# A gated convolution and an ELU feed-forward layer on one core: the last rows of w_in are loaded once and doubled by TensorE

## The chip, the cores and the metric

The kernel runs on one NeuronCore of a Trainium2 chip. The metric is the device time of one execution in microseconds (us); lower is better. The engines are named as in the profile: PE (TensorE: matrix products; PEld is its loading of weights), DVE (VectorE), ACT (ScalarE), POOL (GpSimd) and SP (SyncE, which here only issues DMAs; SPq is its queue). SBUF is the memory that the engines work on, PSUM the one that TensorE writes into.

## The reference

```python
# 4 x 4096 tokens of 192 features, 8 heads of 24 features, 7 taps
w = softmax(weight_gen, axis=-1)          # [B, S, 8, 7], sum + 1e-9
out[b, s, h] = sum_k w[b, s, h, k] * x_pad[b, s + k, h]      # causal, 24 features a head
h = out.reshape(16384, 192) @ w_in        # [192, 2048], float64 in memory
g = where(h > 0, h, exp(min(h, 0)) - 1)   # ELU
return (g @ w_out).astype(float32)        # [2048, 192], float64 in memory
```

So each token's features are averaged over seven places with its own softmaxed weights, and the result goes through two matrix products with an ELU between them.

## The kernel before

**Blocks and tiles.** The 16384 tokens are cut into 32 blocks of 512. A block's convolution gives a 192 x 512 matrix (features by tokens, after transposes). The 192 features lie in four quarters of 48; of each quarter the first 32 rows ("A") fill 128 partitions, and the last 16 rows ("D") of the four quarters make 64 rows, which are held twice, so that they fill 128 partitions as well. The hidden dimension of 2048 is cut into 16 f-tiles of 128.

**Split numbers.** Each factor is split into a high and a low part (hi, lo) that TensorE multiplies in one pass each. For one f-tile, `f_tile` issues five matmuls of 512 columns into the PSUM tile h (L467: D lo by xd, A lo by x hi, A hi by x lo, D hi by xd, A hi by x hi), then ScalarE and VectorE form the ELU and split it (L474 relu, L476 exp, L478 VectorE's add and max into h, L481 hi, L483 lo, which is the last reader of h), and five more matmuls add the tile's share of the result into the PSUM tiles acc and accd (L496). The doubled D rows carry the token's hi part against one copy and its lo part against the other (`second`, L450 and L453: xr and xd).

**Weights.** w_in and w_out come as 64-bit floats, two 32-bit words each. `weights(f0, nf)` handles a piece: first two pieces of one f-tile, then seven of two ("pairs"). SP loads it into the tile raw: one DMA for the A rows (L297), four for the D rows of the four quarters, each written to two places (L299), one for w_out (L302). ScalarE takes the absolute value of the upper words (L308) and scales the lower ones (L311), VectorE clamps, shifts and ors (L314, L317, L320), GpSimd adds the lower words (L323): the tile m is then float32. ScalarE casts it into W as the hi part (L325, L327), GpSimd subtracts for the lo part (L334). All weights stay in W.

**Convolution.** `chunk` loads inputs and softmaxes the tap weights. Blocks 0 and 1 are summed by TensorE: VectorE makes seven products v (L390) and TensorE adds them with an identity matrix in plain float32 (L419). Later blocks are made by GpSimd alone (seven products, six sums; the last writes xc), and VectorE transposes the result (L444) and forms xlo and xd (L453).

**What sets the order.** The code first records every task with an engine, a cost and a due time (`Plan.add`), and then a list scheduler (`Plan.issue`) simulates the engines and writes the instructions out in that order; each engine runs its own in the order written. A ring is a fixed number of buffers (h has 4, raw 4, m 3), and a task that takes a buffer waits until the previous holder's readers are through. The runs are block 0 with tiles 0 to 7, block 1 with 0 to 7, both with 8 to 15, then block 2 to 31 with all sixteen.

```python
runs = [(0, 0, NF2), (1, 0, NF2), (0, NF2, NF), (1, NF2, NF)]
runs += [(blk, 0, NF) for blk in range(2, NB)]
```

The names that the change touches: `weights`, the layout of W (A_HI ... D_LO), the rings raw, m and h, `f_tile` (which weights it waits for) and the constants at the start.

Of the kernel before, what the change touches and what calls it, by code (L numbers as in the profile page):

```python
# [141 lines left out]
def conv_elu_kernel(  # L142
# [38 lines left out]
    def rows(ap, t0, n):  # L181
# [26 lines left out]
    r_wm = ring("wm", [P, CM, H, 1], 1)  # L210
# [46 lines left out]
    def due1(s):  # L257
        return T0 + s * STEP
# [4 lines left out]

    def weights(f0, nf):
        raw, m, hi_h, lo_h = r_raw.new(), r_m.new(), Handle(), Handle()
        for f in range(f0, f0 + nf):
            w_h[f] = (hi_h, lo_h)
        n = nf * WC

        ni = 2 * nf * P  # L270

        def inputs(ap):
            return ap.rearrange("p (c f m) -> p c f m", c=2, f=nf)

        def outputs(ap):
            return ap.rearrange("p (f m) -> p f m", f=nf)

        def m_(c=slice(0, n)):
            return m.t[:, c]

        def mf(c=slice(0, n)):
            return m_(c).bitcast(F32)

        def word(i):
            return raw.t[:, 0:n, i]

        w_in, w_out = slice(0, ni), slice(ni, n)
        fs = W[:, f0:f0 + nf]
        in_hi = fs[:, :, 0:2 * P].rearrange("p f (c m) -> p c f m", c=2)
        in_lo = fs[:, :, A_LO.start:D_LO.stop].rearrange("p f (c m) -> p c f m", c=2)  # L290
        out_hi = fs[:, :, 2 * P:WC]

        def load():
            w = moe_w_in.bitcast(I32).rearrange("(q e) m -> q e m", q=Q)[
                :, :, 2 * f0 * P:2 * (f0 + nf) * P]
            r = raw.t[:, 0:n].rearrange("p c w -> p (c w)")
# [28 lines left out]
        add("act", act(ni), lambda: nc.scalar.copy(out=in_hi, in_=inputs(mf(w_in))),  # L325
            reads=[m], writes=[hi_h])
        add("act", act(n - ni), lambda: nc.scalar.copy(out=out_hi, in_=outputs(mf(w_out))),  # L327
            reads=[m], writes=[hi_h])
        for c, src, hi, lo in ((ni, lambda: inputs(mf(w_in)), in_hi, in_lo),
                               (nf * P, lambda: outputs(mf(w_out))[:, :, 0:P], fs[:, :, O_HI],  # L330
                                fs[:, :, O_LO]),
                               (nf * D1, lambda: outputs(mf(w_out))[:, :, P:D],
                                fs[:, :, O_BOTH.start:WC], fs[:, :, WC:O_BOTH.stop])):
            add("pool", pool(c), lambda src=src, hi=hi, lo=lo: nc.gpsimd.tensor_tensor(  # L334
                out=lo, in0=src(), in1=hi.bitcast(F32), op=ALU.subtract),
                reads=[m, hi_h], writes=[lo_h])

    xw_h, wg_h = {}, {}
# [118 lines left out]
    acc_h = {}  # L457

    def f_tile(blk, f, s, first, last):
        whi, wlo = w_h[f]  # L460
        xhi, xlo, xd, _ = xt_h[blk]
        h, e, hi, lo = r_h.new(), r_e.new(), r_hi.new(), r_lo.new()

# [29 lines left out]
        def mm2():  # L493
# [4 lines left out]
                    stop=(last and r is lo), skip_group_check=True,  # L498
                )

        add("pe", 5 * pe(N), mm2, reads=[whi, wlo, hi, lo], writes=[acc, accd],
            due=due1(s + LA) + 5 * pe(N))

    def drain(blk, s1):
# [30 lines left out]
    with tc.manual_schedule():  # L535

        nc.vector.memset(scratch, 0.0)
        nc.scalar.activation(out=scratch, in_=scratch, func=ACTF.Exp)
        make_identity(nc, ident)
        nc.gpsimd.iota(count, pattern=[[0, 1]], base=0, channel_multiplier=1)  # L540
        nc.vector.tensor_scalar(out=count, in0=count, scalar1=4, scalar2=1,
                                op0=ALU.logical_shift_right, op1=ALU.bitwise_and)
        nc.vector.tensor_copy(out=second, in_=count)
        s = 0
        for blk, f0, f1 in runs:
            c, j0 = chunk_of[blk]
# [46 lines left out]
```

## Time and profile before

| | |
|---|---|
| median of 3 runs | 1252.93 us (1252.63 to 1255.36) |
| the profiled execution | 1255.2 us, of which its span 1253.4 us |
| PE busy | 1200.1 us (96%) |
| DVE, ACT, POOL busy | 897.8, 914.8, 711.5 us (72%, 73%, 57%) |
| mean granted TensorE clock | 0.979 of full speed |

The span runs from the first instruction to the last; the execution's time holds some 2 us around it. Durations in the profile come from one execution. In a row of a timeline, the first number is the start in us from the span's start, the second the duration, and a bracket at the end gives the idle time of the engine before it and what ended it.

### The profile page before, as it was taken

The numbers are of one execution on the slowest core, as the hardware profiler recorded it, in microseconds if no ns is written. First come the engines' busy times: TensorE is split into PE (matmuls) and PEld (weight loads), VectorE is DVE, ScalarE is ACT, GpSimd is POOL, SyncE is SP. The second block draws the span as 40 slices with busy tenths as digits, with TensorE's granted clock in tenths as the row PEclk, the third lists the DMA queues.
The fourth block names the chain that finished last, engine by engine and source line by source line (L and its number), as shares of the span: only waits on it lengthen the run. The fifth ranks groups of instructions, "written<-read, shape, count | busy, mean of one in ns | idle before, by whom it ended". The sixth has DMA issues, their size and how long they took to land.

```text
span 1253.4 us, 15492 instructions
## 1 busy us (share of the span) xinstructions
PE 1200.1 (96%) x5176; PEld 980.1 (78%) x5176; DVE 897.8 (72%) x1398; ACT 914.8 (73%) x1687; POOL 711.5 (57%) x433
## 2 busy tenths in 40 slices
PE   3479999999999999999999999999999999999997
PEld 2248788788888888888888888888888888888886
DVE  5368878888778777676676777667776666666664
ACT  2258677778877777777777777777777777777775
POOL 2235999979999965646676464667656555000000
PEclk9679999999999999999999999999999999999999
DMA  4453040413331404030400403040140000000000
GB/s 102 106 101 44 15 49 13 50 14 45 42 40 24 51 13 51 13 38 13 50 13 13 50 14 44 7 51 13 15 49 13 7 7 13 13 13 13 13 14 13
DMA packets 252364, 39.69 MB, mean 32 GB/s; under 512 B 247932, under 2 KB 250492, under 8 KB 252284
## 3 DMA queue, kind: packets, MB, share of 16 engines
q1 hardware_dynamic: 252284, 38.70, 22.3%
q8 instruction: 40, 0.66, 0.2%
q14 instruction: 40, 0.33, 0.1%
HBM read 26.10 MB, written 12.58 MB: 31 GB/s over the span
## 4 chain that ended last, share of the span: by engine, by line
PE 88%; DMA 4%; SPq 3%; DVE 2%; ACT 2%; issue 1%; POOL 0%; ACTq 0%; POOLq 0%; DVEq 0%
PE h L467 44%; PE acc L496 26%; PE accd L496 18%; DMA raw<-in_moe_w_in 2%; SPq L359 2%; DMA raw<-in_moe_w_out 1%; ACT e L474 0%; SPq L299 0%; ACT e L476 0%; DVE h L478 0%; ACT hi L481 0%; DVE lo L483 0%; SPq L297 0%; POOL m L323 0%; SPq L302 0%
## 5 line engine op out<-in xcount | busy, mean ns | idle before, releaser
L483 DVE TENSOR_TENSOR lo<-h,hi 128x512 fp32r<-128x512 f32 x512 | 350.4, 684 | 291.3 <-ACT hi L481 284.9
L474 ACT ACTIVATE e<-h 128x512 f32<-128x512 f32 x512 | 305.9, 598 | 220.1 <-PE h L467 217.9
L467 PE MATMUL h<-xd,W 128*128 128x512 f32 x1024 | 403.9, 394 | 13.0 <-DVE xd L453 12.0
L496 PE MATMUL acc<-hi,W 128*128 128x512 f32 x1024 | 400.7, 391 | 15.7 <-ACT hi L481 15.7
L467 PE MATMUL h<-xhi,W 128*128 128x512 f32 x1024 | 401.4, 392 | 0.0
L478 DVE SCALAR_TENSOR_TENSOR h<-e,h 128x512 f32<-128x512 f32 x512 | 350.3, 685 | 21.9 <-ACT e L476 21.7
L481 ACT CAST hi<-h 128x512 fp32r<-128x512 f32 x512 | 298.3, 583 | 45.1 <-DVE h L478 43.3
L476 ACT ACTIVATE e<-e 128x512 f32<-128x512 f32 x512 | 329.1, 643 | 1.8
L390 POOL TENSOR_TENSOR pb<-xw,wg 128x768 f32<-128x768 f32 x180 | 284.6, 1581 | 13.9
L405 POOL TENSOR_TENSOR pa<-pa,pb 128x768 f32<-128x768 f32 x150 | 281.1, 1874 | 9.4
L467 PEld LDWEIGHTS h<-xd,W 128*128 128x128 f32 x1024 | 194.3, 190 | 57.1 <-issue 10.8
L496 PEld LDWEIGHTS acc<-hi,W 128*128 128x128 f32 x1024 | 192.9, 188 | 58.4 <-ACT hi L481 18.3
L467 PEld LDWEIGHTS h<-xhi,W 128*128 128x128 f32 x1024 | 194.4, 190 | 40.9 <-issue 0.6
L467 PE MATMUL h<-xlo,W 128*128 128x512 f32 x512 | 200.7, 392 | 0.0
L496 PE MATMUL accd<-lo,W 128*128 128x512 f32 x512 | 200.0, 391 | 0.1
L496 PE MATMUL accd<-hi,W 128*128 128x512 f32 x512 | 199.9, 390 | 0.0
L496 PE MATMUL acc<-lo,W 128*128 128x512 f32 x512 | 199.9, 390 | 0.0
L405 POOL TENSOR_TENSOR xc<-pa,pb 128x768 f32<-128x768 f32 x30 | 55.5, 1850 | 242.5 <-DVE xt L444 146.6
L467 PEld LDWEIGHTS h<-xlo,W 128*128 128x128 f32 x512 | 97.2, 190 | 20.5
L496 PEld LDWEIGHTS accd<-lo,W 128*128 128x128 f32 x512 | 96.5, 188 | 20.9 <-DVE lo L483 0.9
L496 PEld LDWEIGHTS acc<-lo,W 128*128 128x128 f32 x512 | 96.6, 189 | 20.0
L496 PEld LDWEIGHTS accd<-hi,W 128*128 128x128 f32 x512 | 96.4, 188 | 19.9
(45 smaller groups left out, 507.8 us busy)
## 6 DMA issues: line engine op xcount, KB each, us to landing
xw<-in_x SPq DMA_DIRECT2D x60, 228.0 KB
out_dram<-ot SPq DMA_DIRECT2D x128, 64.0 KB
out_dram<-od SPq DMA_DIRECT2D x64, 64.0 KB
wg<-in_weight_gen SPq DMA_DIRECT2D x60, 56.0 KB
raw<-in_moe_w_out SPq DMA_DIRECT2D x7, 384.0 KB
raw<-in_moe_w_in SPq DMA_DIRECT2D x7, 256.0 KB
raw<-in_moe_w_in SPq DMA_DIRECT2D x28, 64.0 KB
xw<-in_x SPq DMA_DIRECT2D x8, 132.0 KB
```

The costliest lines, as they stand in the source:

```text
L359: nc.sync.dma_start(out=to()[q * A:(q + 1) * A], in_=rows(src, t0, n)[:, :, q * d:(q + 1) * d])
L390: lambda: eng.tensor_tensor(out=h.t, in0=xw.t[:, j0 + k:j0 + k + J, :].rearrange("p j (h g) -> p j h g", g=G), in1=wg.t[:, j0:j0 + J, :, k ...
L405: add("pool", pool(J * DQ), lambda b=b, to=to: nc.gpsimd.tensor_tensor(out=to.t, in0=a.t, in1=b.t, op=ALU.add), reads=[b] if to is a else ...
L467: nc.tensor.matmul(out=h.t, lhsT=W[:, f, w], rhs=r.t, start=(i == 0), stop=(i == len(pairs) - 1))
L474: add("act", act(N, True), lambda: nc.scalar.activation(out=e.t, in_=h.t, func=ACTF.Relu, scale=-1.0), reads=[h], writes=[e])
L476: add("act", act(N), lambda: nc.scalar.activation(out=e.t, in_=e.t, func=ACTF.Exp, scale=-1.0), writes=[e])
L478: add("dve", dve(N), lambda: nc.vector.scalar_tensor_tensor(out=h.t, in0=e.t, scalar=-1.0, in1=h.t, op0=ALU.add, op1=ALU.max), reads=[e], ...
L481: add("act", act(N, True), lambda: nc.scalar.copy(out=hi.t, in_=h.t), reads=[h], writes=[hi])
L483: add("dve", dve(N), lambda: nc.vector.tensor_tensor(out=lo.t, in0=h.t, in1=hi.t.bitcast(F32), op=ALU.subtract), reads=[h, hi], writes=[lo])
L496: nc.tensor.matmul(out=to.t, lhsT=W[:, f, w], rhs=r.t, start=(first and r is hi and w != O_LO), stop=(last and r is lo), skip_group_check= ...
```

## The change

The A rows are now loaded by four DMAs, one per quarter, whose outermost size is 32 rows on both sides (L301 of the changed kernel). The D rows of an f-tile are loaded once: the 64 rows of an even tile go to partitions 0 to 63 and those of the odd tile after it to 64 to 127 of the same 128 columns (L307), so piece 0 carries the D rows of tiles 0 and 1, piece 1 none, and each pair its own two. A piece's columns fall from 448 a tile to 320 and 128 more for two tiles' D rows (768 a pair instead of 896). When m is done, TensorE multiplies it with two 0/1 matrices (`picks`), each of which takes one tile's 64 rows to both halves of 128 partitions, into a new PSUM tile wd (L342). ScalarE copies wd into W as the hi part (L346), VectorE subtracts for the lo part (L348). The A and w_out parts are now beside each other in W, so that ScalarE casts them with one instruction (L351) and GpSimd subtracts with two (L356) instead of three. The ring of h falls from 4 buffers to 3, and wd has one. `w_h[f]` lists all handles of a tile's weights, and `f_tile` waits for all of them. The 0/1 matrices are built at the start out of two iotas.

```diff
-    A_HI, D_HI, O_HI, O_BOTH, A_LO, D_LO, O_LO = (
-        slice(c, c + P) for c in (0, P, 2 * P, 3 * P, WC + D1, WC + D1 + P, WC + D1 + 2 * P))
+    D_HI, A_HI, O_HI, O_BOTH, A_LO, O_LO, D_LO = (slice(c, c + P) for c in range(0, 7 * P, P))
...
-    r_raw = ring("raw", [P, 2 * WC, 2], 4, I32)
-    r_m = ring("m", [P, 2 * WC], 3, I32)
+    MC = P + 2 * (P + D)
+    r_raw = ring("raw", [P, MC, 2], 4, I32)
+    r_m = ring("m", [P, MC], 3, I32)
...
-    r_h = ring("h", [P, N], 4, pool=ps)
+    r_h = ring("h", [P, N], 3, pool=ps)
+    r_wd = ring("wd", [P, 2, P], 1, pool=ps)
...
+        AO = P + D
+        na = nf * AO
+        n = na + (0 if f0 % 2 else P)
...
-            nc.sync.dma_start(out=r[:, 0:ni], in_=w[:, 0:A])
             for q in range(Q):
                 nc.sync.dma_start(
-                    out=r[q * A:(q + 1) * A, ni:2 * ni],
-                    in_=w[q, A:DQ].unsqueeze(0).to_broadcast([2, E, ni]))
+                    out=r[q * A:(q + 1) * A, :, 0:2 * P],
+                    in_=w[q, 0:A, cols].rearrange("e (f m) -> e f m", f=nf))
+            if n > na:
+                for i in range(2):
+                    cols = slice(2 * (f0 + i) * P, 2 * (f0 + i + 1) * P)
+                    nc.sync.dma_start(
+                        out=raw.t[i * D1:(i + 1) * D1, na:n].rearrange("p c w -> p (c w)"),
+                        in_=w[:, A:DQ, cols])
...
+        if n > na:
+            wd, d_hi, d_lo = r_wd.new(), Handle(), Handle()
+            for f in (f0, f0 + 1):
+                w_h.setdefault(f, []).extend((d_hi, d_lo))
+            ds = W[:, f0:f0 + 2]
+
+            def pick():
+                for i in range(2):
+                    nc.tensor.matmul(out=wd.t[:, i], lhsT=picks[i], rhs=mf(slice(na, n)),
+                                     start=True, stop=True)
+
+            add("pe", 2 * 4 * pe(P), pick, reads=[m], writes=[wd], due=due1(f0) - 2000)
+            add("act", act(2 * P, True), lambda: nc.scalar.copy(out=ds[:, :, D_HI], in_=wd.t),
+                reads=[wd], writes=[d_hi])
+            add("dve", dve(2 * P), lambda: nc.vector.tensor_tensor(
+                out=ds[:, :, D_LO], in0=wd.t, in1=ds[:, :, D_HI].bitcast(F32), op=ALU.subtract),
+                reads=[wd, d_hi], writes=[d_lo])
+        add("act", act(na), lambda: nc.scalar.copy(out=ao_hi, in_=ao(slice(0, AO))),
             reads=[m], writes=[hi_h])
...
-        add("pe", 5 * pe(N), mm1, reads=[whi, wlo, xhi, xlo, xd], writes=[h], due=due1(s))
+        add("pe", 5 * pe(N), mm1, reads=[*ws, xhi, xlo, xd], writes=[h], due=due1(s))
...
+        for i, p in enumerate(picks):
+            own = slice(i * D1, (i + 1) * D1)
+            nc.vector.memset(p, 0.0)
+            nc.vector.tensor_scalar(out=p[own], in0=col[own], scalar1=row[own], scalar2=None,
+                                    op0=ALU.is_equal)
```

The order of the instructions comes from the scheduler. On SP, at the program's start, the inputs of block 0's convolution (wg, xw) and then the first piece of the weights stood like this before:

```order
L359 DMA wg<-in_weight_gen 32x16x14 x4
L359 DMA xw<-in_x 32x22x48 x4
L297 DMA raw<-in_moe_w_in 128x1x256
L299 DMA raw<-in_moe_w_in 32x1x256 x4
L302 DMA raw<-in_moe_w_out 128x384
```

And now, on the same engine at the same place, with the pair that follows:

```order
L381 DMA wg<-in_weight_gen 32x16x14 x4
L381 DMA xw<-in_x 32x22x48 x4
L301 DMA raw<-in_moe_w_in 32x256 x4
L307 DMA raw<-in_moe_w_in 64x1x256 x2
L310 DMA raw<-in_moe_w_out 128x384
L301 DMA raw<-in_moe_w_in 32x2x256 x4
```

The loads stay in their place behind the inputs of block 0; one DMA of 128 rows and four of 32 became four of 32 and two of 64.

On TensorE, at the end of block 0's seven taps (v: a tap's product; acc, accd: where they are summed), the rows before were these, with the first f-tile behind them:

```order
L419 MATMUL acc_110<-v_145,ident_64 128x384
L419 MATMUL accd_111<-v_145,ident_64 128x384
L419 MATMUL acc_110<-v_154,ident_64 128x384
L419 MATMUL accd_111<-v_154,ident_64 128x384
L467 MATMUL h_209<-xd_204,W_68 128x512
L467 MATMUL h_209<-xhi_189,W_68 128x512
```

Now the picks of the first two pieces with D rows (wd: the doubled rows) stand between and behind the last taps:

```order
L441 MATMUL acc_125<-v_145,ident_64 128x384
L441 MATMUL accd_126<-v_145,ident_64 128x384
L342 MATMUL wd_169<-m_147,pick0_72 128x128
L342 MATMUL wd_169<-m_147,pick1_73 128x128
L441 MATMUL acc_125<-v_154,ident_64 128x384
L441 MATMUL accd_126<-v_154,ident_64 128x384
L441 MATMUL acc_125<-v_166,ident_64 128x384
L441 MATMUL accd_126<-v_166,ident_64 128x384
L342 MATMUL wd_211<-m_172,pick0_72 128x128
L342 MATMUL wd_211<-m_172,pick1_73 128x128
L489 MATMUL h_227<-xd_221,W_74 128x512
```

TensorE thus comes to the last two taps only after GpSimd has finished m of piece 0, and to the first f-tile only after m of the first pair.

## Rows read from the trace of the kernel before

**Rows 1.** The page: TensorE's busy time, share of the span and instructions with the other engines', and its busy share in 40 equal slices of the span, in tenths.

```profile
PE 1200.1 (96%) x5176; PEld 980.1 (78%) x5176; DVE 897.8 (72%) x1398; ACT 914.8 (73%) x1687; POOL 711.5 (57%) x433
...
PE   3479999999999999999999999999999999999997
```

**Rows 2.** Stretches of the span: from and to in us, length, then busy us and instructions of PE, PEld, DVE, ACT and POOL, the granted TensorE clock as a share of full speed, the mean busy share of the 16 DMA engines, and GB/s.

```profile
0.00:28.00 28.00, 12.32 (x28) 6.72 (x28) 14.04 (x26) 5.55 (x10) 5.27 (x12) 0.96 0.42 98
28.00:155.00 127.00, 96.82 (x349) 71.92 (x349) 86.72 (x127) 76.96 (x137) 69.33 (x50) 0.82 0.35 69
...
100.00:120.00 20.00, 20.00 (x89) 16.54 (x89) 19.80 (x31) 18.39 (x35) 8.55 (x7) 1.00 0.44 54
...
155.00:1253.00 1098.00, 1090.95 (x4800) 901.49 (x4800) 796.99 (x1247) 832.24 (x1541) 636.93 (x373) 1.00 0.21 26
```

**Rows 3.** The chain of waits in order of time, of the first 160 us: start us, length us, what it was.

```profile
10.81 9.42 DMA raw<-in_moe_w_in
...
46.13 12.30 DMA raw<-in_moe_w_in
...
100.44 1.13 PE h L467 x5
...
120.06 2.48 POOL m L323
...
149.25 1.30 DVE xt L444 x2
...
154.93 4.06 PE h L467 x10
```

**Rows 4.** The timeline of SP's queue: start, duration of the issue, line and transfer, count of DMAs.

```profile
0.74 1.97 SPq L359 DMA_DIRECT2D wg<-in_weight_gen  x4
2.75 2.17 SPq L359 DMA_DIRECT2D xw<-in_x  x4
...
5.75 2.60 SPq L299 DMA_DIRECT2D raw<-in_moe_w_in  x4
8.39 0.41 SPq L302 DMA_DIRECT2D raw<-in_moe_w_out  x1
...
13.72 5.93 SPq L299 DMA_DIRECT2D raw<-in_moe_w_in  x4
...
90.45 0.41 SPq L302 DMA_DIRECT2D raw<-in_moe_w_out  x1
```

**Rows 5.** Short stretches within the loads, columns as in rows 2: only broadcast loads; broadcast loads and a load of A rows; a load of w_out beside broadcasts.

```profile
17.00:20.00 3.00, 3.00 (x11) 1.80 (x10) 2.13 (x3) 0.00 (x0) 1.60 (x1) 1.00 0.13 49
...
54.00:56.00 2.00, 2.00 (x8) 1.16 (x8) 0.00 (x0) 0.00 (x0) 0.00 (x0) 1.00 0.26 87
...
28.00:29.00 1.00, 0.00 (x0) 0.00 (x0) 0.76 (x2) 1.00 (x3) 1.00 (x1) 0.50 0.93 303
```

**Rows 6.** Groups of instructions by line and shape in the first 155 us: busy us, mean ns of one, idle time before them and what ended it.

```profile
L323 POOL TENSOR_TENSOR m<-m,raw 128x896 int32<-128x896 int32 x7 | 16.6, 2365 | 24.6 <-DVE m L320 24.6
...
L334 POOL TENSOR_TENSOR W<-m,W 128x512 fp32r<-128x512 f32 x7 | 9.7, 1384 | 26.8 <-ACT W L325 26.8
L320 DVE SCALAR_TENSOR_TENSOR m<-raw,m 128x896 int32<-128x896 int32 x7 | 8.6, 1224 | 0.0
...
L334 POOL TENSOR_TENSOR W<-m,W 128x128 fp32r<-128x128 f32 x9 | 7.4, 823 | 0.0
```

**Rows 7.** Waits of GpSimd in the first 155 us: who waited for whom, us in total, times, longest.

```profile
POOL m L323 <- DVE m L320: 27.0, 7, 7.9
```

**Rows 8.** The timelines of TensorE, GpSimd and VectorE at the start.

```profile
17.86 0.81 PE L419 MATMUL acc<-v,ident 128*128 128x384 f32 x2
18.51 0.81 PE L419 MATMUL accd<-v,ident 128*128 128x384 f32 x2
...
31.50 0.77 PE L467 MATMUL h<-xd,W 128*128 128x512 f32 x1 [9.60 <-DVE xd L453]
...
18.40 1.74 POOL L323 TENSOR_TENSOR m<-m,raw 128x448 int32<-128x448 int32 x1 [17.01 <-DMA raw<-in_moe_w_in]
...
24.02 0.63 DVE L314 TENSOR_SCALAR m<-m 128x896 f32<-128x896 f32 x1 [4.88 <-ACT m L308]
```

**Rows 9.** The timeline in the steady part: the first matmul of a tile, VectorE's last read of that tile's h, and the first matmul of the third tile after it.

```profile
600.80 0.39 PE L467 MATMUL h<-xd,W 128*128 128x512 f32 x1
...
605.51 0.69 DVE L483 TENSOR_TENSOR lo<-h,hi 128x512 fp32r<-128x512 f32 x1 [0.98 <-ACT hi L481]
...
607.60 0.39 PE L467 MATMUL h<-xd,W 128*128 128x512 f32 x1
```

**Rows 10.** The timelines of TensorE and of VectorE around 230 us, where VectorE makes xlo and xd of the next block: the first matmuls of three tiles, VectorE's two operations and its read of h.

```profile
225.50 0.39 PE L467 MATMUL h<-xd,W 128*128 128x512 f32 x1
...
232.29 0.39 PE L467 MATMUL h<-xd,W 128*128 128x512 f32 x1
...
235.48 0.50 PE L467 MATMUL h<-xd,W 128*128 128x512 f32 x1 [0.75 <-DVE lo L483]
...
230.51 2.36 DVE L453 TENSOR_TENSOR xlo<-xt,xhi 128x512 fp32r<-128x512 f32 x1
232.79 2.03 DVE L453 TENSOR_TENSOR xd<-xt,xr 128x512 fp32r<-128x512 f32 x1
234.74 0.68 DVE L483 TENSOR_TENSOR lo<-h,hi 128x512 fp32r<-128x512 f32 x1
```

More of the change, by code (lines that the diff above doesn't have):

```diff
@@ L193, in conv_elu_kernel @@
     second = const.tile([P, 1], F32, name="second")
+    row = const.tile([P, 1], F32, name="row")
+    rows_i = const.tile([P, 1], I32, name="rows_i")
+    ids = const.tile([P, P], I32, name="ids")
+    col = const.tile([P, P], F32, name="col")
+    picks = [const.tile([P, P], F32, name=f"pick{i}") for i in range(2)]
     WC = 2 * P + D
     W = const.tile([P, NF, 2 * WC], F32R, name="W")
-    A_HI, D_HI, O_HI, O_BOTH, A_LO, D_LO, O_LO = (
-        slice(c, c + P) for c in (0, P, 2 * P, 3 * P, WC + D1, WC + D1 + P, WC + D1 + 2 * P))
+    D_HI, A_HI, O_HI, O_BOTH, A_LO, O_LO, D_LO = (slice(c, c + P) for c in range(0, 7 * P, P))
     pieces = [(0, 1), (1, 1)] + [(f, 2) for f in range(2, NF, 2)]
@@ L265, in weights @@
         raw, m, hi_h, lo_h = r_raw.new(), r_m.new(), Handle(), Handle()
+        AO = P + D
+        na = nf * AO
+        n = na + (0 if f0 % 2 else P)
         for f in range(f0, f0 + nf):
[L267 to L276, printed above, removed]
+            w_h.setdefault(f, []).extend((hi_h, lo_h))
         def m_(c=slice(0, n)):
@@ L282, in mf, with ao @@
             return m_(c).bitcast(F32)
+        def ao(c):
+            return mf(slice(0, na)).rearrange("p (f m) -> p f m", f=nf)[:, :, c]
         def word(i):
             return raw.t[:, 0:n, i]
-        w_in, w_out = slice(0, ni), slice(ni, n)
         fs = W[:, f0:f0 + nf]
-        in_hi = fs[:, :, 0:2 * P].rearrange("p f (c m) -> p c f m", c=2)
-        in_lo = fs[:, :, A_LO.start:D_LO.stop].rearrange("p f (c m) -> p c f m", c=2)
-        out_hi = fs[:, :, 2 * P:WC]
+        ao_hi = fs[:, :, A_HI.start:WC]
         def load():
-            w = moe_w_in.bitcast(I32).rearrange("(q e) m -> q e m", q=Q)[
-                :, :, 2 * f0 * P:2 * (f0 + nf) * P]
-            r = raw.t[:, 0:n].rearrange("p c w -> p (c w)")
-            nc.sync.dma_start(out=r[:, 0:ni], in_=w[:, 0:A])
+            w = moe_w_in.bitcast(I32).rearrange("(q e) m -> q e m", q=Q)
+            r = raw.t[:, 0:na].rearrange("p (f m) w -> p f (m w)", f=nf)
+            cols = slice(2 * f0 * P, 2 * (f0 + nf) * P)
             for q in range(Q):
                 nc.sync.dma_start(
-                    out=r[q * A:(q + 1) * A, ni:2 * ni],
-                    in_=w[q, A:DQ].unsqueeze(0).to_broadcast([2, E, ni]))
+                    out=r[q * A:(q + 1) * A, :, 0:2 * P],
[6 more added lines that the diff above has]
+                        in_=w[:, A:DQ, cols])
             nc.sync.dma_start(
-                out=r[:, 2 * ni:2 * n].rearrange("p (f m) -> p f m", f=nf),
+                out=r[:, :, 2 * P:2 * AO],
                 in_=moe_w_out.bitcast(I32)[f0 * P:(f0 + nf) * P, :].rearrange(
                     "(f p) m -> p f m", p=P))
-        add("dma", max(dma(2 * P, 8 * nf * P) + dma(nf * P, 8 * D), 6 * ISSUE), load, writes=[raw])
+        add("dma", max(dma((nf + 1) * P, 8 * P) + dma(nf * P, 8 * D), 7 * ISSUE), load,
+            writes=[raw])
         add("act", act(n), lambda: nc.scalar.activation(
@@ L324, in weights @@
             out=m_(), in0=m_(), in1=word(0), op=ALU.add), reads=[raw, tail], writes=[m])
-        add("act", act(ni), lambda: nc.scalar.copy(out=in_hi, in_=inputs(mf(w_in))),
-            reads=[m], writes=[hi_h])
[L327 to L335, printed above, removed]
+        if n > na:
[14 more added lines that the diff above has]
+        add("act", act(na), lambda: nc.scalar.copy(out=ao_hi, in_=ao(slice(0, AO))),
+            reads=[m], writes=[hi_h])
+        for c, hi, lo in ((slice(0, 2 * P), slice(P, 3 * P), slice(A_LO.start, O_LO.stop)),
+                          (slice(2 * P, AO), slice(3 * P, WC), slice(WC, O_BOTH.stop))):
+            add("pool", pool(nf * (c.stop - c.start)), lambda c=c, hi=hi, lo=lo:
+                nc.gpsimd.tensor_tensor(
+                    out=fs[:, :, lo], in0=ao(c), in1=fs[:, :, hi].bitcast(F32), op=ALU.subtract),
                 reads=[m, hi_h], writes=[lo_h])
@@ L459, in f_tile @@
     def f_tile(blk, f, s, first, last):
[L460 removed]
+        ws = w_h[f]
         xhi, xlo, xd, _ = xt_h[blk]
@@ L499, in mm2 @@
                 )
-        add("pe", 5 * pe(N), mm2, reads=[whi, wlo, hi, lo], writes=[acc, accd],
+        add("pe", 5 * pe(N), mm2, reads=[*ws, hi, lo], writes=[acc, accd],
             due=due1(s + LA) + 5 * pe(N))
@@ L540, in conv_elu_kernel @@
         nc.gpsimd.iota(count, pattern=[[0, 1]], base=0, channel_multiplier=1)
+        nc.gpsimd.iota(ids, pattern=[[E, Q], [0, 2], [1, E]], base=0, channel_multiplier=0)
+        nc.vector.tensor_scalar(out=rows_i, in0=count, scalar1=D1 - 1, scalar2=None,
+                                op0=ALU.bitwise_and)
+        nc.vector.tensor_copy(out=row, in_=rows_i)
         nc.vector.tensor_scalar(out=count, in0=count, scalar1=4, scalar2=1,
@@ L543, in conv_elu_kernel @@
         nc.vector.tensor_copy(out=second, in_=count)
+        nc.vector.tensor_copy(out=col, in_=ids)
+        for i, p in enumerate(picks):
[3 more added lines that the diff above has]
+                                    op0=ALU.is_equal)
         s = 0
```

## The prediction

> **What bounds the kernel now.** I read the page first: TensorE is busy 96% of the span, and its slices show where the other 4% is: the first five slices, some 155 us, are not full, and after them every slice is [rows 1]. The stretches say the same in numbers: from 155 us to the end TensorE is busy 1090.95 of 1098 us at the full clock, while in the 155 us before it is busy 12.32 + 96.82 us, and its granted clock averages 0.82 from 28 us on, that is, part of that time it ran at the lower of its two levels [rows 2]. So only the start can give time back, and the change touches only the start, with one exception (the buffers of h, below). In the chain of waits the start hangs on the weight loads (9.42 and 12.30 us are two of them), then on TensorE's groups of five matmuls at 1.13 us, and at the end on the last weight piece on GpSimd (120.06), after which GpSimd makes the convolution of block 2, whose result VectorE transposes at 149.25 [rows 3]. Block 2's first matmul is at 154.93, when both first blocks are done; I call this time T2. Everything after T2 is 4,800 matmuls back to back [rows 2], so what T2 gains, the end gains.
>
> Why the loads are slow is in the DMA share. While only the broadcast loads of the 16 last rows run, the share is 0.13 of 16 engines, 2 engines' worth, and 49 GB/s; with the 128-row load of w_in beside them 0.26 and 87 GB/s; a stretch with w_out's load has 0.93 and 303 GB/s [rows 5]. The queue feels it: four broadcasts of a pair took 5.93 us to issue where four took 2.60 us undisturbed, and the last weight load was issued only at 90.45 [rows 4].
>
> **The change, part by part.** A pair is a piece of two f-tiles; there are seven, and two pieces of one tile.
>
> Loads. Per pair 256 KB in one DMA, 4 x 64 KB of broadcasts and 384 KB of w_out become 256 KB in four DMAs, 2 x 64 KB without broadcast, and 384 KB. Issue at undisturbed prices [rows 4]: 2.60 (four) + 2 x 0.65 + 0.41 = 4.3 us per pair; the first piece the same, the other single 3.0. All weights: 4.3 + 3.0 + 7 x 4.3 = 37.4 us; with block 1's convolution inputs (1.97 + 2.17) ahead of the last of them, SP is done at 4.9 + 41.5 = 46 us where it was 91. Transfer, bounded by [rows 5]: w_out 393 KB at 303 GB/s is 1.3 us; the 256 KB 0.9 us at 303 to 3.0 us at 87; the last rows' 131 KB 0.4 us at 303 to 2.7 us at 49. That is 2.6 to 7.0 us a pair; I take 3.6, since the four 32-row loads look like w_out's (many rows outermost), the others like neither. Issue then sets the pace; by the upper end the last pair lands some 15 us later, near 61 us. TensorE uses a pair for 2 tiles x 2 blocks x 2.26 = 9.1 us, so even 7.0 feeds it.
>
> The share of 0.13 for a source that repeats 2 times 16 rows is told by the Trainium skill too, "DMA: Bandwidth & Descriptors", section on why a DMA increments its semaphore by 16: a DMA runs on the largest number of engines up to 16 that divides the outermost sizes of both its sides. The trace agrees (2 of 16 is 0.125). By that rule the new 64-row loads, whose source still begins with 4 quarters, run on 4 engines and not on 16, which speaks against this part of the change; the pair would land in an estimated 0.9 + 1.5 + 1.3 = 3.7 us, still under the issue.
>
> GpSimd. Per pair the sum shrinks from 896 to 768 columns (2.365 us to 2.03 in proportion) and the three subtractions become two, of 512 (1.384) and 128 (0.823) [rows 6]: 4.2 us a pair, 7 x 4.2 + about 5 for the singles = 35 us. ScalarE's two conversions shrink by a seventh too, and get a copy of 256 columns from PSUM; I set this to nothing: its 76.96 us from 28 to 155 us are 10 less than VectorE's [rows 2].
>
> VectorE. The or-step falls from 1.224 us by a seventh, seven times, 1.2 us; the two shorter steps I leave. Added: eight subtractions of 256 columns out of PSUM, each between 0.35 (1.224 x 256/896, rows 6) and 0.69 us (a 512-column subtraction, [rows 9]): 2.8 to 5.5; I take 3.3, near the size-scaled row. The eight tiny operations that make the 0/1 matrices run before 5 us, where VectorE has nothing (1 us if not hidden).
>
> TensorE. 16 picks of 128 columns in plain float32. The nearest rows are the 384-column ones, 0.645 us apart [rows 8]; a third is 0.21, so 3.4 us, at most 16 x 0.645 = 10.3. What a pick holds up behind it is a rival.
>
> The first matmul of a tile. At 31.50 it had waited 9.60 us for xd, which VectorE made late because at 24.02 it was itself waiting for ScalarE's first pass over a pair, that is for its load [rows 8]. Now that load is issued by 13.5 us, but ScalarE first casts piece 0, which GpSimd ends at 20.14 (18.40 + 1.74, the same work on 448 columns as before); then the pair's pass gives VectorE its work at about 21.5, 2.5 us earlier. First tile: 31.5 - 2.5 - (smaller steps) = 28.5.
>
> Order. On SP nothing moves past these loads; a piece with last rows has seven issues for six. On TensorE the pick of piece 0 stands ahead of block 0's last two taps and waits for GpSimd until 20.14, where these taps ran on at 18 us: 2 us, hidden, since the transposes behind them wait for VectorE till 24.
>
> T2. TensorE: 28.5 + 64 groups x 1.13 [rows 3] = 72.3, + block 1's 14 tap matmuls x 0.645 = 9.0, + 3.4 = 113. VectorE: busy 86.72 us from 28 to 155 [rows 2], + 3.3 - 1.2 = 89, so not before 117 even without a pause; it can nearly do that (19.80 of 20 us from 100 to 120, with TensorE full beside it). GpSimd: the last sum came 29 us after the last load's issue (90.9 to 120.06); 46 + 29 = 75, + 2.5, + 27 for the convolution (122.5 to 149.25) = 105, so this chain loses the end by 10 us. I take T2 = 117 + 3 for what the engines wait on each other = 120, 35 us earlier; 113 to 128.
>
> h's ring goes from 4 buffers to 3, since wd takes a PSUM bank. This lasts all run. The matmuls of tile s + 3 now wait until VectorE has read h of tile s. In the steady part that read ends at 605.51 + 0.69 = 606.20 for the tile begun at 600.80, and tile s + 3 starts at 607.60: 1.4 us to spare [rows 9]. Where VectorE is held up it fails: at 230.51 and 232.79 two operations of 512 columns took 2.36 and 2.03 us, the read for the tile begun at 225.50 ended at 235.42, and tile s + 3 had started at 232.29; four buffers cost 0.75 us there [rows 10], three would cost 3.1. I charge 3 us in all (0 to 10): such a place in the blocks just after T2, none later.
>
> Sum: -35 + 3 = -32 us. The profiled execution took 1255.2 us (span 1253.4); 1223 for it, and 2.3 us less, 1221, against the median of 1252.93.
>
> **Rivals.** (1) Picks hold TensorE. Each stands in its queue and waits for a sum on GpSimd, which in turn waited for VectorE 27.0 us over seven pieces [rows 7]. If TensorE waits 2.5 us at each of the six later picks, T2 is 135: 1237. For: the picks stand between tiles in TensorE's queue. Against: picks are due early, and tiles ahead of them fill the time. (2) VectorE's work shrinks more than counted, since its steps beside GpSimd's shorter ones are less held up, and h costs nothing: T2 = 113, 1211. (3) Little gained: the new loads still run at 49 to 87 GB/s and block each other in the queue, or the last convolution remains last because its inputs are issued after all weights; T2 above 145, 1243 to 1253, say 1249. Against: [rows 5] and 10 us of spare. (4) Slower: h's ring. If the hold-up of [rows 10] comes in every one of the 30 later blocks, each costs 3.1 - 0.75 = 2.4 us: 72 us, 1221 - 3 + 72 = 1290. It decides from 15 blocks on. For: each block has these two operations. Against: 4,800 matmuls took 1098 us, and the steady rows have 1.4 us spare. The Trainium skill has a rule for it ("SBUF — State Buffer", who interferes with whom): a VectorE operation with two SBUF inputs and a GpSimd operation that reads SBUF lock each other out of a shared port. The trace agrees (2.36 us against 0.68 for the same size with one input in PSUM, rows 10); by the rule alone every block is at risk while GpSimd works.
>
> **How the numbers follow.** Forecast 0.62 (1213 to 1231), (1) 0.14, (2) 0.09, (3) 0.09, (4) 0.06. The range 1208 to 1241 leaves out (4), most of (3), and tails. A measurement here tells 0.2%, 2.5 us, from no change. Faster: 0.62 + 0.14 + 0.09 + half of (3) = 0.89; same 0.05; slower 0.06.
>
> **What would show it.** Right: no stretch at a share of 0.13 before 50 us; SP's last weight issue near 46; first tile near 28.5; TensorE at full clock from about 50 us; block 2's first matmul near 120, VectorE over 90% busy from 28 to there. Wrong: TensorE waiting on m at L342 for over 10 us in all (1), VectorE's lo ending waits of h at L489 block after block (4), the convolution's xc ending the wait at T2 (3).

## The result, and the profile after

The changed kernel took 1222.89 us (median of 4 runs, 1222.09 to 1223.2) against 1254.0 (1252.63 to 1255.36) of the kernel before, timed beside it: a ratio of 0.9751, 95% interval 0.9734 to 0.9768, 31.1 us less. The forecast was 1221, the range 1208 to 1241. The profiled execution took 1223.0 us, its span 1221.1, which is 32.3 us under the span of before. Of all the executions below one stands apart, the profiled one of the kernel with four shared buffers of h: it took 3129.15 us where its three others took 1217.52 to 1219.53, so no row of it is used.

The page of the changed kernel, the lines of [rows 1]:

```profile
PE 1191.8 (98%) x5208; PEld 975.3 (80%) x5208; DVE 894.3 (73%) x1413; ACT 909.9 (75%) x1686; POOL 699.9 (57%) x425
...
PE   5899999999999999999999999999999999999997
```

Where four of TensorE's slices stood under nine tenths, three do now, one of them the last in both. TensorE's busy time fell by only 8.3 us, though it does more (5208 matmuls for 5176, by the picks): fewer of them ran at the lower clock (the mean granted clock is 0.998 where it was 0.979). The rest of the gain, some 24 us, is idle time of TensorE that is gone.

Stretches of the changed kernel, columns as in [rows 2]: short ones in the loads and at the first tile, then from the start to the first tile, from there to block 2's first matmul (T2 in the prediction), and from T2 to the end.

```profile
15.00:20.00 5.00, 3.82 (x13) 2.01 (x13) 3.63 (x6) 0.30 (x1) 1.73 (x1) 1.00 0.66 128
...
20.00:28.00 8.00, 4.01 (x17) 2.41 (x17) 6.94 (x15) 5.28 (x10) 3.65 (x4) 0.97 0.93 164
28.00:31.00 3.00, 3.00 (x8) 2.35 (x9) 1.58 (x5) 1.46 (x4) 3.00 (x5) 0.50 0.53 137
...
50.00:100.00 50.00, 46.83 (x208) 37.34 (x207) 45.41 (x74) 41.26 (x78) 32.97 (x23) 1.00 0.50 62
...
0.00:27.72 27.72, 12.73 (x37) 7.14 (x37) 17.89 (x40) 8.57 (x15) 6.10 (x13) 1.00 0.73 138
27.72:119.36 91.64, 84.10 (x353) 64.77 (x353) 81.16 (x123) 69.65 (x126) 62.19 (x43) 0.98 0.42 71
119.36:1221.10 1101.74, 1095.00 (x4820) 903.39 (x4820) 795.26 (x1252) 831.69 (x1545) 631.56 (x371) 1.00 0.20 26
```

The DMA engines are at 0.66 and 128 GB/s from 15 to 20 us, where [rows 5] had 0.13 and 49 GB/s from 17 to 20. The clock is full from 50 us on; of the stretches shown, only the one at the first tile is at the lower level (0.50). From the first tile to T2 TensorE is busy 92% of the time and VectorE 89%.

The timelines of the changed kernel: TensorE at the first two picks, the first tile and T2; VectorE ahead of T2; GpSimd's end of block 2's convolution and what it does next to VectorE's xlo and xd.

```profile
19.72 0.71 PE L342 MATMUL wd<-m,pick 128*128 128x128 f32 x4 [1.18 <-POOL m L332]
25.57 0.71 PE L342 MATMUL wd<-m,pick 128*128 128x128 f32 x4 [2.55 <-POOL m L332]
27.72 0.80 PE L489 MATMUL h<-xd,W 128*128 128x512 f32 x1 [1.44 <-DVE xd L475]
...
119.36 0.50 PE L489 MATMUL h<-xd,W 128*128 128x512 f32 x1 [1.40 <-DVE lo L505]
...
114.89 1.56 DVE L475 TENSOR_TENSOR xlo<-xt,xhi 128x512 fp32r<-128x512 f32 x1
116.37 2.33 DVE L475 TENSOR_TENSOR xd<-xt,xr 128x512 fp32r<-128x512 f32 x1
118.62 0.68 DVE L505 TENSOR_TENSOR lo<-h,hi 128x512 fp32r<-128x512 f32 x1
...
107.46 1.85 POOL L427 TENSOR_TENSOR xc<-pa,pb 128x768 f32<-128x768 f32 x1
...
115.98 2.17 POOL L427 TENSOR_TENSOR pa<-pa,pb 128x768 f32<-128x768 f32 x1
```

The first tile is at 27.72 (31.50 in [rows 8]), T2 at 119.36 (154.93 in [rows 3]). What ends the wait at T2 is lo, the last reader of an h buffer; xd had ended 0.66 us before it (116.37 + 2.33 = 118.70), and lo stood behind xd in VectorE's queue. GpSimd had finished the convolution at 109.31.

T2 is 35.6 us earlier, though the span is only 32.3 shorter. The difference is in what stands ahead of T2. One group of matmuls up to T2, of the changed kernel:

```profile
L518 PE MATMUL acc<-hi,W 128*128 128x512 f32 x56 | 22.5, 402 | 0.0
```

and the same of the kernel before, up to its T2, with the stretch behind it:

```profile
L496 PE MATMUL acc<-hi,W 128*128 128x512 f32 x64 | 27.2, 426 | 15.7 <-ACT hi L481 15.7
```

```profile
154.93:1253.40 1098.47, 1091.02 (x4800) 901.56 (x4800) 797.06 (x1247) 832.24 (x1541) 637.00 (x373) 1.00 0.21 26
```

A tile has two of these acc matmuls in its second group. Before, 32 tiles had them ahead of T2, now 28: four groups of five matmuls, the 20 by which 4820 exceeds 4800, were taken behind T2. At 0.2266 us a matmul (1.133 for a group of five) that is 4.5 us. For equal work T2 is at 119.36 + 4.53 = 123.9, 31.0 us earlier, and what follows takes 1101.74 - 4.53 = 1097.2, 1.3 us less than before (a difference of two effects, as the last experiment shows). I use this measure for T2 below and call it T2 for equal work.

SP's queue in the changed kernel, columns as in [rows 4]: the first pair's loads, then the last issue ahead of the long pause, and the first and the last issue of the pair behind it.

```profile
8.99 1.84 SPq L301 DMA_DIRECT2D raw<-in_moe_w_in  x4
10.87 1.14 SPq L307 DMA_DIRECT2D raw<-in_moe_w_in  x2
12.06 0.45 SPq L310 DMA_DIRECT2D raw<-in_moe_w_out  x1
...
41.70 0.39 SPq L310 DMA_DIRECT2D raw<-in_moe_w_out  x1
48.47 2.65 SPq L301 DMA_DIRECT2D raw<-in_moe_w_in  x4
...
52.36 0.48 SPq L310 DMA_DIRECT2D raw<-in_moe_w_out  x1
```

The first pair takes 1.84 + 1.14 + 0.45 = 3.4 us to issue, the others up to 4.3, and nothing holds a weight load's issue up as the 5.93 us of [rows 4] did. From 42.1 to 48.5 SP stands with one pair to go.

All that TensorE waited for in the changed kernel (us in total, times, longest), and the groups by shape in its first 122 us (columns as in [rows 6]):

```profile
PE acc L441 <- DVE v L412: 11.1, 3, 9.8
PE wd L342 <- POOL m L332: 5.3, 4, 2.6
PE h L489 <- DVE lo L505: 4.9, 4, 1.7
PE h L489 <- DVE xd L475: 1.4, 1, 1.4
```

```profile
L332 POOL TENSOR_TENSOR m<-m,raw 128x768 int32<-128x768 int32 x7 | 13.8, 1968 | 13.8 <-ACT e L496 4.2 <-DVE m L329 3.8 <-ACT raw L320 2.4
L356 POOL TENSOR_TENSOR W<-m,W 128x512 fp32r<-128x512 f32 x7 | 10.2, 1461 | 13.6 <-ACT W L351 13.6
...
L356 POOL TENSOR_TENSOR W<-m,W 128x128 fp32r<-128x128 f32 x7 | 5.4, 777 | 0.0
L342 PE MATMUL wd<-m,pick 128*128 128x128 f32 x32 | 5.3, 287 | 5.3 <-POOL m L332 5.3
```

### The profile page after: what moved, and what is told of

It reads as the page before. It is cut to its first block, busy times and chain, and to the rows that moved or that the text cites. A ratio compares the mean times of both kernels' runs of the same rounds, so it can differ in the third digit from the quotient of the medians.

```text
span 1221.1 us, 15642 instructions
## 1 busy us (share of the span) xinstructions
PE 1191.8 (98%) x5208; PEld 975.3 (80%) x5208; DVE 894.3 (73%) x1413; ACT 909.9 (75%) x1686; POOL 699.9 (57%) x425
## 4 chain that ended last, share of the span: by engine, by line
PE 93%; SPq 2%; DMA 2%; issue 1%; DVE 1%; POOL 0%; ACT 0%; DVEq 0%; POOLq 0%
PE h L489 46%; PE acc L518 28%; PE accd L518 19%; SPq L301 1%; DMA raw<-in_moe_w_out 1%; SPq L381 1%; DMA raw<-in_moe_w_in 1%; SPq L307 0%; POOL m L332 0%; DMA xw<-in_x 0%; DVE h L500 0%; DVE lo L505 0%; SPq L310 0%; DVE m L326 0%; PE wd L342 0%
```

## The experiments

Theory 1: the gain is the loads, which no longer run on two of the 16 DMA engines; the doubling on TensorE is only the means. Its rivals: the gain comes from the smaller columns (an eighth or a seventh less for the engines that prepare the weights); or the picks and the smaller ring of h give a part of it back. Each time is a median, and each ratio is against the kernel before, timed beside it.

**A rows in four DMAs, broadcasts kept.** The kernel before, with

```diff
-            nc.sync.dma_start(out=r[:, 0:ni], in_=w[:, 0:A])
+            for q in range(Q):
+                nc.sync.dma_start(out=r[q * A:(q + 1) * A, 0:ni], in_=w[q, 0:A])
```

> The kernel before, with w_in's A rows alone loaded by four DMAs of 32 rows instead of one of 128; the D rows are broadcast as before. Theory 1 (the gain is the loads' spread over the DMA engines, and the broadcasts are the larger part): the broadcasts still run at a DMA share of 0.13; a pair still needs some 6 to 7 us of the busiest engines instead of 8, so block 2's first matmul comes about 8 to 12 us earlier than 154.9 and the kernel takes 1240 to 1248 us. Theory 2 (the gain is the smaller work of 768 columns instead of 896 on VectorE, ScalarE and GpSimd): no change within 0.2%, 1252 to 1256 us.

1246.17 us (ratio 0.9929, 0.9907 to 0.995), 8 us less; T2 moved from 154.93 to 147.22. A quarter of the gain.

**The broadcasts spread as well.** The same, with the 16 rows outermost in place of the repetition (and the tokens' rows in the same order, so that the result is the same):

```diff
-                    in_=w[q, A:DQ].unsqueeze(0).to_broadcast([2, E, ni]))
+                    in_=w[q, A:DQ].unsqueeze(1).to_broadcast([E, 2, ni]))
...
-                        src = src[:, :, A:DQ].unsqueeze(2).to_broadcast([P, n, 2, E])
+                        src = src[:, :, A:DQ].unsqueeze(3).to_broadcast([P, n, E, 2])
...
-        nc.vector.tensor_scalar(out=count, in0=count, scalar1=4, scalar2=1,
+        nc.vector.tensor_scalar(out=count, in0=count, scalar1=0, scalar2=1,
```

> The kernel before with both loads of w_in spread and nothing else: A rows by four DMAs of 32 rows, and the D rows' broadcasts with their 16 rows outermost and the copy inside (the two copies of a row lie beside each other, in weights and tokens alike); still 896 columns, h's ring of 4, no picks, nine DMAs a pair. Theory 1: nearly the whole gain, no stretch at a share of 0.13, block 2's first matmul at 119 to 126 us, 1221 to 1229 us. Theory 2: at most a third of the gain, 1243 us or more.

1227.54 us (0.9789, 0.9771 to 0.9806), 26.7 us less. No picks, the old column counts, the old ring of h. The timeline of TensorE at T2, and the stretch behind T2:

```profile
128.74 0.50 PE L468 MATMUL h<-xd,W 128*128 128x512 f32 x1 [2.57 <-DVE xd L454]
```

```profile
128.74:1227.00 1098.26, 1091.03 (x4800) 901.58 (x4800) 797.03 (x1247) 830.65 (x1541) 636.65 (x373) 1.00 0.20 26
```

T2 is 26.2 us earlier, and what follows takes what it took before, 1098.3 us. So the order of one access pattern's dimensions is worth 18.6 us beyond the step above, and Theory 1 has most of the gain.

**The ring of h alone.** The kernel before, with

```diff
-    r_h = ring("h", [P, N], 4, pool=ps)
+    r_h = ring("h", [P, N], 3, pool=ps)
```

> The kernel before with h's ring cut from 4 buffers to 3. My account: a stall where VectorE's xlo and xd are held up, in a few blocks after block 2, as at 232.29 (3.1 us there): 2 to 6 us longer, 1256 to 1260 us. Rival 4 of the prediction: a stall of some 2.4 us in every one of 30 blocks, 1310 us or more. A third possibility: the scheduler writes another order and nothing is lost, 1252 to 1255 us.

1264.25 us (1.0081, 1.0061 to 1.0102), 10 us more, above what I expected and far below the rival. TensorE's waits for h, and the stretch behind T2:

```profile
PE h L467 <- DVE lo L483: 10.8, 11, 3.1
```

```profile
157.27:1264.60 1107.33, 1096.64 (x4815) 904.83 (x4815) 794.56 (x1250) 830.97 (x1543) 634.70 (x372) 1.00 0.21 25
```

15 matmuls are behind T2 here (3.4 us), so T2 for equal work is 160.7, 5.7 us late, and the rest takes 1103.9, 5.5 us longer. Eleven waits, not one in each of 30 blocks. In the changed kernel the same ring has four such waits of 4.9 us in all, and it costs some 2.3 us behind T2 (shown with the last experiment). Part of the difference can be seen in the trace: two of the waits, 1.41 us at 186.68 and 1.81 us at 191.09, are followed by a fall of the clock, 0.83 on the mean from 190 to 200 us, which the changed kernel does not have. Why the kernel before waits more often was not settled.

**Four buffers of h in the changed kernel**, wd taken from the same ring:

```diff
-    r_h = ring("h", [P, N], 3, pool=ps)
-    r_wd = ring("wd", [P, 2, P], 1, pool=ps)
+    r_h = ring("h", [P, N], 4, pool=ps)
...
-            wd, d_hi, d_lo = r_wd.new(), Handle(), Handle()
+            wd, d_hi, d_lo = r_h.new(), Handle(), Handle()
```

> The changed kernel with h's ring back at 4 buffers; the doubled rows take their turn in that ring instead of having a PSUM tile of their own. If the ring of 3 costs what the trace shows (TensorE's waits for lo of 4.5 us in the first 130 us, one of 0.8 us later): 1 to 4 us shorter, 1219 to 1222 us. If the ring is free because VectorE sets block 2's start: 1222 to 1224 us.

1219.52 us (0.9719, 0.9701 to 0.9738), 3.4 us less than the changed kernel. The three kernels give the parts of the gain: spread loads -26.7, the doubling with its smaller columns and fewer issues -8.0 (1227.54 to 1219.52), the ring of h +3.4. Which of the three in the middle term gives how much was not separated.

**D loads with 16 rows outermost** in the changed kernel:

```diff
-                        in_=w[:, A:DQ, cols])
+                        in_=w[:, A:DQ, cols].rearrange("q e m -> e q m"))
...
-        nc.gpsimd.iota(ids, pattern=[[E, Q], [0, 2], [1, E]], base=0, channel_multiplier=0)
+        nc.gpsimd.iota(ids, pattern=[[1, Q], [0, 2], [Q, E]], base=0, channel_multiplier=0)
```

> The changed kernel with one change: the D rows' loads take the 16 rows outermost and the four quarters inside, and the 0/1 matrices are made for that order. My account (issue and the raw ring set the loads' pace, the D rows' transfer lies under it): nothing to tell, 1221 to 1224 us, though the low DMA shares of 0.25 to 0.3 in which only D loads run should go. If the slow D loads hold the first tiles back: 1217 to 1221 us.

1223.02 us (0.9751, 0.973 to 0.9772): no difference. T2 119.37.

**A rows in one DMA of 128 rows per tile** in the changed kernel:

```diff
-            for q in range(Q):
+            for j in range(nf):
                 nc.sync.dma_start(
-                    out=r[q * A:(q + 1) * A, :, 0:2 * P],
-                    in_=w[q, 0:A, cols].rearrange("e (f m) -> e f m", f=nf))
+                    out=r[:, j, 0:2 * P],
+                    in_=w[:, 0:A, 2 * (f0 + j) * P:2 * (f0 + j + 1) * P])
```

> The changed kernel with w_in's A rows loaded as before with the four quarters outermost, one DMA of 128 rows a tile, the D rows and the doubling as in the changed kernel. If the spread of the A rows matters beside the D rows: a pair needs about 2.4 us of four engines for A and 1.5 for D, 4 to 5 us with w_out, above the issue of 2.9; the loads end near where they do now, since the raw ring holds them anyway, and the first tile comes about 1 us later: 1222 to 1226 us. If the A rows' spread were half of the gain, as their share in bytes: 1232 to 1240 us.

1223.98 us (0.9756, 0.9739 to 0.9774), 1.1 us more; T2 120.45, 1.1 us later. Once the broadcasts are gone, the number of outermost rows of the other loads, each changed alone, decides 1 us or nothing. The 1.1 us go with the clock: from 57 to 60 and from 60 to 63 us it was 0.87 and 0.56 here, and 1.00 in the changed kernel.

**Picks that wait for nothing, and their place with it.** In the changed kernel

```diff
-                    nc.tensor.matmul(out=wd.t[:, i], lhsT=picks[i], rhs=mf(slice(na, n)),
+                    nc.tensor.matmul(out=wd.t[:, i], lhsT=picks[i], rhs=col,
...
-            add("pe", 2 * 4 * pe(P), pick, reads=[m], writes=[wd], due=due1(f0) - 2000)
+            add("pe", 2 * 4 * pe(P), pick, reads=[], writes=[wd], due=due1(f0) - 2000)
```

> The changed kernel with the picks reading a constant tile instead of m, so that they wait for nothing and the scheduler puts them, and the copies out of PSUM, at the start; the last 16 rows' weights are left out of the result by this, all else is computed. It bounds what the picks cost by their waits and their place. My account (TensorE's 5.3 us of waits on m are partly hidden): 1 to 4 us less than the changed kernel, 1219 to 1222 us. Rival 1 of the prediction (picks hold the tiles behind them by 2.5 us each): 8 to 15 us less, 1208 to 1215 us. Costing nothing: 1222 to 1224 us.

1228.24 us (0.9793, 0.9772 to 0.9814), 5.3 us more, which neither theory expected. The timeline of TensorE:

```profile
2.66 1.26 PE L342 MATMUL wd<-col,pick 128*128 128x128 f32 x4 [2.66 <-DVE pick L574]
...
33.16 0.80 PE L489 MATMUL h<-xd,W 128*128 128x512 f32 x1 [6.96 <-DVE xd L475]
```

The edit changed more than the wait: with nothing to read, the scheduler put all picks and their copies at the start, and the first tile came at 33.16 in place of 27.72. It says nothing on the waits, so I made the next two.

**Picks that don't wait for GpSimd, in their old place.** Only the operand is exchanged (`rhs=col`); `reads=[m]` stays, so the order stays.

> The changed kernel with one operand exchanged: the picks multiply the constant matrix col instead of m, and the order of all instructions stays as it is. It leaves out the doubled last rows: the weights made of them are wrong numbers. TensorE then waits at the picks for wd's single buffer alone and no more for GpSimd's sum; in the changed kernel it waited 5.3 us there in four places, 2.6 us at most. Theory 1 (TensorE's own work sets block 2's start, since it is busy 88 of the 96 us from the first tile to there): the waits behind the first tile are won back, block 2's first matmul comes 2 to 4 us before 119.4, 1219 to 1221 us. Rival (VectorE and the ring of h set it, the waits at the picks are hidden): block 2's first matmul within 1 us of 119.4, 1222 to 1224 us.

1222.98 us (0.9743, 0.9729 to 0.9758): no difference in the time, the rival's number. TensorE's timeline at the first tile's pick, the first tile and T2, and the stretch from the first tile to T2:

```profile
23.06 0.71 PE L342 MATMUL wd<-col,pick 128*128 128x128 f32 x4 [1.13 <-DVE W L348]
28.09 0.79 PE L489 MATMUL h<-xd,W 128*128 128x512 f32 x1 [4.31 <-DVE xd L475]
...
119.68 0.50 PE L489 MATMUL h<-xd,W 128*128 128x512 f32 x1 [1.10 <-DVE lo L505]
...
28.09:119.68 91.59, 85.69 (x353) 66.32 (x353) 80.38 (x123) 69.71 (x126) 62.00 (x43) 0.96 0.43 70
```

The pick came 2.5 us earlier and the first tile no earlier: TensorE waited longer for xd instead (4.31 in place of 1.44). Taking the waits at the picks away won no time, but this does not show that they cost nothing, because the clock differed. For the same 353 matmuls TensorE was busy 85.69 us where it had been 84.10; it idled 5.9 us, 1.6 less than in the changed kernel, and a lower clock (0.96 for 0.98) took the 1.6 us back. Beside the stretch at the first tile, the clock was 0.86 and 0.58 from 57 to 60 and from 60 to 63 us. The mean clock was lower in all four executions (0.994 to 0.996; 0.996 to 0.998 in the changed kernel). Whether the fall belongs to the edit is open: the kernel with 128-row loads, whose picks do wait, shows it in the same place.

**Every pick three times** (`for i in (0, 0, 0, 1, 1, 1)`):

> The changed kernel with every pick issued three times in the place of once (the same result each time), the order otherwise as it is. The picks held TensorE busy 5.3 us in all, so this adds 10.6 us to TensorE before block 2. Theory 1 (TensorE's own work sets block 2's start): all of it but what falls into the waits of the first 28 us (two of eight pairs, 2.6 us) shows, 6 to 9 us, 1229 to 1232 us. Rival (VectorE and the ring of h set it, TensorE has room): under 3 us, 1222 to 1226 us.

1223.88 us (0.9754, 0.9738 to 0.9771), 1 us more, again the rival's. The first tile, the third-last pick and T2 on TensorE, then VectorE and GpSimd ahead of T2, and the two stretches around the first tile:

```profile
27.23 0.50 PE L489 MATMUL h<-xd,W 128*128 128x512 f32 x1 [0.55 <-DVE xd L475]
...
63.72 1.60 PE L342 MATMUL wd<-m,pick 128*128 128x128 f32 x12 [1.40 <-POOL m L332]
...
119.19 0.39 PE L489 MATMUL h<-xd,W 128*128 128x512 f32 x1
...
116.28 0.67 DVE L475 TENSOR_TENSOR xlo<-xt,xhi 128x512 fp32r<-128x512 f32 x1
116.88 0.67 DVE L475 TENSOR_TENSOR xd<-xt,xr 128x512 fp32r<-128x512 f32 x1
...
116.34 2.93 POOL L427 TENSOR_TENSOR pa<-pa,pb 128x768 f32<-128x768 f32 x1
```

```profile
20.00:28.00 8.00, 5.77 (x31) 4.07 (x30) 7.42 (x16) 4.84 (x10) 3.86 (x5) 1.00 1.03 164
28.00:31.00 3.00, 2.53 (x11) 1.77 (x10) 2.11 (x7) 2.97 (x6) 2.71 (x4) 1.00 0.76 196
```

A pair's picks take 1.60 us in place of 0.71, 7.1 us over the eight, less than the 10.6 I had set. T2 is not later, with the same 28 groups ahead of it. The two first ones, 1.8 us, lie in waits; from 28 to 31 us the clock stayed full, where half of it had been granted, 1.5 us; and the waits of 1.74 us at 58.60 and 1.40 at T2 are gone. These make 6.4 us. One profile each does not tell how much of that is chance (the clock, and who waits at T2), but 7 us of work on TensorE showed as 1.

**All that helped or might**: four shared buffers of h, D loads with 16 rows outermost, and a raw ring of 5 instead of 4.

> The changed kernel with three changes: h's ring of 4 shared with the doubled rows, D loads with 16 rows outermost, and raw's ring 5 instead of 4, so that SP no longer stands from 42 to 48 us waiting for a free raw. Measured so far for the shared ring alone: 1219.5 us. If SP's stand delays the inputs of block 2's convolution and this the start of block 2: 1 to 3 us less than that, 1216.5 to 1218.5 us. If TensorE's own work sets the start by now: 1218.5 to 1220.5 us.

1218.17 us (1217.38 to 1218.88; 0.9712, 0.9693 to 0.973), the fastest of all, 4.7 us under the changed kernel. The last weight issue is at 45.70. T2, and the stretch behind it:

```profile
117.50 0.50 PE L488 MATMUL h<-xd,W 128*128 128x512 f32 x1 [1.26 <-DVE xd L474]
```

```profile
117.50:1215.70 1098.20, 1091.89 (x4815) 903.56 (x4815) 794.87 (x1251) 833.73 (x1544) 633.86 (x371) 1.00 0.19 26
```

15 matmuls more than before behind T2: for equal work T2 is 120.9 and the rest 1094.8. Against the changed kernel that is 3.0 us ahead of T2 and 2.4 behind it. Against the ring of four alone (1219.52) it is 1.4 us less, and the single times of the two overlap (1217.38 to 1218.88, 1217.52 to 1219.53), so the other two changes are not shown to give anything.

The 400 us behind T2 show what the ring does there. In order: the kernel before (four buffers), the changed one (three), this one (four); then the first 6 us behind T2 of the kernel before.

```profile
154.93:554.93 400.00, 398.99 (x1748) 328.88 (x1749) 313.59 (x475) 309.68 (x569) 329.17 (x191) 1.00 0.29 35
119.36:519.36 400.00, 399.60 (x1754) 328.31 (x1755) 308.54 (x474) 307.65 (x568) 323.94 (x189) 1.00 0.28 34
117.50:517.50 400.00, 400.00 (x1764) 330.98 (x1765) 311.36 (x479) 311.64 (x573) 326.04 (x189) 1.00 0.28 35
154.93:160.93 6.00, 6.00 (x19) 4.77 (x20) 3.17 (x6) 3.12 (x6) 5.76 (x4) 0.72 0.44 66
```

With three buffers TensorE gets through 10 matmuls fewer than here, 2.3 us; later the two run alike (2648 and 2649 matmuls in the next 600 us). With the 16-row loads alone and three buffers it is 1754 as well, so those are not the cause; a raw ring of 5 was not run alone. The kernel before, with its four buffers, is 16 behind this one, 3.6 us, for another reason in part: right behind T2 its clock was 0.72 and it did 19 matmuls in 6 us, where the changed kernel did 26 at 1.00, 1.6 us. So the 1.3 us that the changed kernel seems to win behind T2 are some 3.7 won against the kernel before, less 2.4 lost again, which I put down to the ring.

## Why the prediction was right, point by point

- **Only the start can give time back.** Right in the main. (The digits of [rows 1] show three slices at the start under nine tenths, and the last one, where the prediction read five; the stretches of [rows 2] carry the point.) Behind T2, for equal work, every profile used here but that of the kernel before with three buffers of h lies between 1094.8 and 1098.5 us; so up to 3.7 us lay there, which the prediction put at nothing.
- **What T2 gains, the end gains.** Wrong by 4.5 us. The sum took 64 groups at 1.13 us ahead of T2 because there were so many before; the changed order has 60 there. T2 was 119.36 where 120 was forecast, but for equal work it was 123.9, 4 us late, inside 113 to 128.
- **h's ring, +3 us in the blocks after T2.** Near, in place and in size: the changed kernel takes 2.4 us longer behind T2 than the one with all three changes, which has four buffers. The ring of four won 3.4 us in all, so it seems to cost something ahead of T2 too, where [rows 10] did not look. Against the kernel before, this loss can't be seen, because that kernel took 3.7 us more behind T2 than it takes with four buffers now, 1.6 of them at the lower clock. No term of the sum had that.
- **The total.** -31.0 at T2, -3.7 and +2.4 behind it make -32.3; the sum had -35 + 3 = -32. T2 was 4 us short, and a gain that nobody forecast made up for it: that the total came so near is luck.
- **The loads.** The cause is shown: 26.7 of 31.1 us come back by spreading the same loads. Issue was set at 4.3 us a pair and was 3.4 to 4.3; the last weight issue was set near 46 and was 52.36, because SP stood for a raw buffer from 42.1 to 48.5, which the sum of issue times left out (with five raw buffers: 45.70). Nothing waited for that pair, so it cost little. The Trainium skill's rule in "DMA: Bandwidth & Descriptors" (the section on why a DMA increments its semaphore by 16), by which the new 64-row loads still run on 4 engines, made no difference to the time: 16 rows outermost gave 1223.02 against 1222.89. The trace is in keeping with the rule: the median time from issue to landing of w_in's 64 KB loads (A and D together) fell from 3.2 to 2.3 us, and the time stayed.
- **GpSimd, 35 us of weights.** 7 x (1.968 + 1.461 + 0.777) = 29.4, and 4.4 for the single tiles: 33.8. Block 2's convolution was done at 109.3 where 105 was forecast, still 10 us before T2.
- **VectorE.** Eight subtractions took 3.3 us, as set. Its share from the first tile to T2 was 89% where over 90% was to be seen, and the bound of 117 was set too late. It laid 89 us of work behind 28 us; but VectorE had done 17.89 us of work by 27.72, where it had done 14.04 by 28 in [rows 2], and from there to T2 it did 81.16. With all three changes T2 came at 117.50.
- **TensorE.** The picks took 5.3 us in place of 3.4 (each is two records of 0.287 us; a third of the 384-column interval was too little), inside the 10.3. The first tile was at 27.72 (28.5). The first pick waited 1.18 us (2 forecast), the second 2.55.
- **The rivals.** (1) TensorE did wait on m, 5.3 us, far from the 2.5 us at each of six picks that the rival needed; taking the waits away won no time, though at a lower clock. (2) VectorE was 89% busy and T2 not at 113. (3) xc was 10 us early, and the loads were not slow. (4) Four waits for h in all.
- **What T2 waits for.** The forecast named VectorE, plus 3 us for what the engines wait on each other. Neither is shown to set it alone: TensorE was idle 7.5 of the 91.6 us, VectorE 10.5, and both removing TensorE's waits at the picks (at a lower clock) and adding 7 us to its work (at a full one) left T2 within 0.4 us of where it was. What would bring it forward much further was not tried.

## What to carry to other kernels

Look first at the DMA share of a stretch in which one kind of load runs alone; a share of 2/16 with a broadcast outermost in the source asks for another order of its dimensions, which here gave 18.6 us, and 26.7 with the A rows spread as well, without any of the doubling. When the time to some marker is summed from the work ahead of it, count in the new order that the same work stands ahead; a smaller ring can move it behind (15 matmuls in the kernel before with three buffers of h). A wait that one reads in a profile (5.3 us at the picks) is worth nothing until a kernel without it, in the same order and at the same clock, is faster.

## What the runs showed that I had not expected

- Who pays when GpSimd and VectorE meet changes from run to run. In the changed kernel VectorE's xlo and xd took 1.56 and 2.33 us beside GpSimd's sum of 2.17; with tripled picks they took 0.67 each, and GpSimd's sum 2.93. In both the engine that began second paid: GpSimd's operations began at 114.35 and 115.98, ahead of xlo (114.89) and xd (116.37); with tripled picks xlo began at 116.28 and GpSimd's sum at 116.34.
- With more work on TensorE its clock did not fall (one profile of each). In the changed kernel it was busy 4.01 us of the 8 before 28 us, and the 3 us after it were granted 0.50, the lower level (1.2 GHz); with tripled picks it was busy 5.77 of 8, and the clock stayed at 1.00.
- Three buffers of h cost 10 us in the kernel before and 3.4 in the changed one.
- A gain behind T2 can hide a loss there: against the kernel before TensorE won 3.7 us there, 1.6 of them by the clock, and 2.4 were lost again with the smaller ring.
